# One run of all four P chunks over eight PSUM banks, and four blocks ahead of the seventh product

## The chip, the cores and the metric

The kernel runs on one core of a Trainium2 chip. The metric is the time of one execution on the device, in microseconds. Five engines work side by side, each on its own queue in order: TensorE (PE, with weight loads shown as PEld), VectorE (DVE), ScalarE (ACT), GpSimd (POOL) and SyncE (SP, which here only issues DMAs).

## The reference

For each of 8 batches and 8 heads, 512 rows of x and 32 rows of state (64 wide) read each other by softmax attention. The 544 result rows per batch, 8 heads side by side (512 wide), go through a two-layer network with an exact Gelu.

```
scores = scale * x @ state.T;   a  = softmax(scores);   xread = a  @ state
scores2 = scale * state @ x.T;  a2 = softmax(scores2);  sread = a2 @ x
h = concat(xread, sread) as (B*544, 512) @ w_in         # w_in 512 x 2048
out = gelu(h) @ w_out                                   # w_out 2048 x 512
```

## The kernel before

The kernel never forms xread. For a batch b it multiplies the state with `w_in` first (P, 128 rows x 2 x 2048), and then `h = a @ P`. The work of a batch is:

- `scores`, `norm`: exponentials and normalized weights `a`; `xtr_dma` and `atr_dma` transpose x and `a` by DMA from the SP queue.
- `p_mm(b, f, tiles)` (line 423): one of four column chunks f of P. It fills two PSUM tiles (t = 0, 1) of 128x512 with 8 matmuls of 64 rows x 32 columns each. `p_copy` (line 438) brings tile 0 to SBUF with ACT (L440) and tile 1 with DVE (L441).
- `mm1` (line 489), called by `M(..)`: one of 16 blocks of h, 2 matmuls of 128x512 (L494) and a Gelu on ACT (L501). "Block 8" is m = 8.
- `X(b, name)` (line 621): one of seven products of a Strassen scheme for `gelu(h) @ w_out`, 16 matmuls of 128x256 each (L591). Products 3 and 5 share PSUM bank 0, products 4 and 2 bank 1, products 1 and 7 bank 2, and product 6 has bank 3. `g_sum` (line 582) makes the sums of blocks that a product needs, on DVE (L585). X3 is copied by ACT (L635), X5 by ACT (L643), X2 by ACT (L648). POOL forms `u` (L646) and `v` (L610) from SBUF. DVE adds `v` and bank 3 (L618), and `u` and X7 (L654); after each of these and after X5 a DMA on SP writes part of the output (L605).
- `sread` (line 386): the state's read of x, 32 small matmuls into one PSUM tile `sr` (L392); `sread_out` normalizes it on DVE straight out of PSUM (L405, L406). `srt` transposes it on PE (L416), and DVE copies it (L419).

PSUM has eight banks: four `f` buffers that go round in the order of allocation (`ftile`, used by h blocks, `sr`, `srT`, scores and P chunks), and four fixed banks `o0` to `o3` (`otile`, used by the products, and by P chunks in between).

The order is written out by hand: each engine's queue holds its instructions in the order of the program text. The main loop (line 1116) runs over batches b = 2 to 7, and in each over eight positions p. A "slot" here is one pass of b. In slots 2 to 6, each p issues blocks 2p and 2p + 1. Products 4, 5, 1, 2, 7 of the previous batch come at p = 0 to 4, and products 3 and 6 of batch b at p = 6 and 7. P of the next batch is made in two runs, chunks 0 and 1 at p = 5 and chunks 2 and 3 at p = 7. In slot 2 two chunks of batch 2's own P are still to be made, by `pmat(2, 2)` at p = 0 and `pmat(2, 3)` at p = 3, in `f` buffers. In slot 6 the reads of batches 6 and 7 are both made. In slot 2, `hold_for` (L912) is a tiny POOL copy that waits for block 12's Gelu before POOL issues the load of x 5.

Of the kernel before, what the change touches and what calls it, by code (L numbers as in the profile page):

```python
# [9 lines left out]
FP32 = mybir.dt.float32  # L10
BF16 = mybir.dt.bfloat16
# [6 lines left out]
def kernel(  # L18
# [36 lines left out]
    def otile(shape, name, at=None):  # L55
        if at is None:
            at = turn[0] % 4
            turn[0] += 1
        return ps_o.tile(shape, FP32, name=name, tag=f"o{at}")

    def ftile(shape, name):
        return ps_f.tile(shape, FP32, name=name, tag="f")
# [323 lines left out]
    def sread(b):  # L386
        A = atts[b]
        A.sr = ftile([128, 2, 65], "sr")
        for t in range(2):
            for j in range(SJ):  # L390
                for c in range(HC):
                    nc.tensor.matmul(  # L392
                        A.sr[32 * c:32 * c + 32, t, :],
                        lhsT=A.e[:, 2 * j + t, 32 * c:32 * c + 32],
                        rhs=A.xo[:, j, c, 1 + 65 * t:66 + 65 * t],
                        start=(j == 0),
                        stop=(j == SJ - 1),
                    )

    def sread_out(b):  # L400
        A = atts[b]
        A.srm = att.tile([128, 2, D], BF16, name="srm", tag="srm")
        flat = A.sr.rearrange("q t d -> q (t d)")
        inv = att.tile([128, 2], FP32, name="inv", tag="inv")
        nc.vector.reciprocal(out=inv, in_=flat[:, 0:130:129])  # L405
        nc.vector.tensor_tensor(  # L406
            out=A.srm,
            in0=flat[:, 1:129].rearrange("q (t d) -> q t d", t=2),
            in1=inv[:, :].to_broadcast((128, 2, D)),
            op=ALU.mult,  # L410
        )
# [26 lines left out]
    def p_copy(b, f, ps):  # L438
        dst = Ps[b][:, :, f * 512:(f + 1) * 512]
        nc.scalar.copy(out=dst[:, 0, :], in_=ps[0])  # L440
        nc.vector.tensor_copy(out=dst[:, 1, :], in_=ps[1])  # L441
# [140 lines left out]
    def g_sum(b, name):  # L582
        (h0, k0), (h1, k1), op = G_SUMS[name]
        t = apool.tile([128, MH, 256], BF16, name="gsum", tag="gsum")
        nc.vector.tensor_tensor(out=t, in0=g_q(b, h0, k0), in1=g_q(b, h1, k1), op=op)  # L585
        xs[b, "g" + name] = t
# [34 lines left out]
    def X(b, name):  # L621
        bank = {"3": 0, "4": 1, "5": 0, "2": 1, "1": 2, "6": 3, "7": 2}[name]
        first = name in "3416"
        if first:
            xs[b, bank] = otile([128, 2, NH], "xp", bank)
        ps = xs[b, bank]
        lhs = {"3": (0, 0), "4": (1, 1)}.get(name)
        lhs = xs[b, "g" + name] if lhs is None else g_q(b, *lhs)
        rhs = {"5": w_q[1][1], "2": w_q[0][0]}.get(name)
        rhs = w_sum[name] if rhs is None else rhs  # L630
        x_mm(ps, lhs, rhs, first)
        if name == "3":
            xs[b, "s3"] = c_tile("s3")
            if b > 1:
                nc.scalar.copy(out=xs[b, "s3"], in_=ps)  # L635
            for h in range(2):
                xs[b, "o", h] = hpool.tile([128, 2, d_model], FP32, name="oh", tag=f"oh{h}")
        elif name == "4":
            xs[b, "s34"] = c_tile("s34")
            nc.vector.tensor_tensor(out=xs[b, "s34"], in0=ps, in1=xs[b, "s3"], op=ALU.add)  # L640
        elif name == "5":
            o = xs[b, "o", 0][:, :, NH:]
            nc.scalar.copy(out=o, in_=ps)  # L643
            xs[b, "u"] = c_tile("u")
            x_out(b, 0, right)
            nc.gpsimd.tensor_tensor(out=xs[b, "u"], in0=xs[b, "s34"], in1=o, op=ALU.subtract)  # L646
        elif name == "2":
            nc.scalar.copy(out=xs[b, "o", 1][:, :, :NH], in_=ps)  # L648
            c22(b)
        elif name == "1":  # L650
            xs[b, "q"] = c_tile("q")
            nc.vector.tensor_tensor(out=xs[b, "q"], in0=ps, in1=xs[b, "s34"], op=ALU.add)
        elif name == "7":
            nc.vector.tensor_tensor(  # L654
                out=xs[b, "o", 0][:, :, :NH], in0=ps, in1=xs[b, "u"], op=ALU.add
            )
            x_out(b, 0, left)
# [88 lines left out]
    def sr_w(name):  # L746
        if name in "52":
            homes = [opool.tile([128, 2, 512], BF16, name="srw", tag="osb") for _ in range(2)]
        elif name == "7":
            t = att.tile([128, 2, 2, 512], BF16, name="srw7", tag="xT")  # L750
            homes = [t[:, 0], t[:, 1]]
        else:
            t = x4s["16".index(name)].rearrange("p j c n -> p (j c n)")
            t = t.rearrange("p (g k f) -> p g k f", g=2, k=2)
            homes = [t[:, 0], t[:, 1]]
        (h0, k0), (h1, k1), op = G_SUMS[name]
        for g in range(2):
            nc.vector.tensor_tensor(
                out=homes[g], in0=sr_wq(h0, k0, g), in1=sr_wq(h1, k1, g), op=op
            )  # L760
            sr["w" + name, g] = homes[g]
# [133 lines left out]
            nc.vector.tensor_tensor(out=rs["o", 0][:, :NH], in0=ps, in1=rs["u"], op=add)  # L895
            r_out(0)

    def p_run(b, fs, banks, copy=None):
        done = []
        for f, at in zip(fs, banks):  # L900
            it = iter(at or ())
            tiles = (lambda shape, name: otile(shape, name, next(it))) if at else ftile
            done.append((b, f, p_mm(b, f, tiles)))
        for x in done:
            (copy or p_copy)(*x)

    def p_copy_v(b, f, ps):
        for t in range(2):
# [207 lines left out]
    for b in range(2, B):  # L1116
        nb = b + 1
        for p in range(8):
            k = 16 * b + 2 * p
            if p == 1 and nb < B:  # L1120
                scores(nb, 0)
                scores(nb, 1)
            if p in (2, 3) and nb < B:
                norm(nb, p - 2)
            if p == 3 and nb + 1 < B:
                xtr_dma(nb + 1)
            if p == 5 and nb < B:
                atr_dma(nb)
            if p == 7 and nb < B:
                srt(b)  # L1130
                if nb == B - 1:
                    srt(nb)
            if nb == B and p < 5:
                read_out_slot(p)
                if p == 4:
                    r_homes()
                    r_sum("5")
                    r_sum("2")
                continue
            M(k, k + 1)  # L1140
            if b == 2 and p in (0, 3):
                pmat(2, 2 + p // 3)
            if b == 2 and p == 1:
                w_sums(4)
            if p < 5:
                if p == 0:
                    g_sum(b - 1, "5")
                    if b > 2:
                        sr_w("5216"[b - 3])
                X(b - 1, "45127"[p])  # L1150
                if p < 3:
                    g_sum(b - 1, "127"[p])
            if p == 0 and b + 3 < B:
                hold_for(b, 0)
                load_x(4 if b == 2 else b + 3)
            if p == 6 and b == 2:
                hold_for(b, 12)
                load_x(5)
            if p == 0 and nb + 1 < B:
                begin(nb + 1)  # L1160
                rearr(nb + 1)
            if nb == B:
                if p == 5:
                    g_sum(b, "6")
                    R("3")
                    r_sum("1")
                    R("4")
                    r_sum("6")
                    r_sum("7")
                if p == 6:  # L1170
                    R("5")
                    X(b, "3")
                    R("2")
                    R("1")
                if p == 7:
                    R("6")
                    X(b, "6")
                continue
            if p == 5:
                g_sum(b, "6")  # L1180
                reads = (b, nb) if nb == B - 1 else (b,)
                for r in reads:
                    sread(r)
                p_run(nb, (0, 1), ((0, 1), (3, 2)))
                for r in reads:
                    sread_out(r)
                if b == 2:
                    rearr_ones(3)
                elif nb + 1 < B:
                    rearr_ones(nb + 1)  # L1190
            if p == 6:
                X(b, "3")
            if p == 7:
                if b == 2:
                    rearr_ones(4)
                p_run(nb, (2, 3), ((1, 2), None))
                X(b, "6")
    b = B - 1
    for name in "521":
# [39 lines left out]
```

## Time and profile before

| | |
|---|---|
| median of 3 runs | 203.81 us (203.44 to 204.97) |
| profiled execution, from the first to the last instruction | 202.5 us |
| PE busy | 196.6 us (97%) |
| DVE busy | 157.1 us (78%) |
| ACT busy | 135.4 us (67%) |
| POOL busy | 67.9 us (34%) |
| granted TensorE clock | 1.000 |
| share of PE in the chain that ended last | 89% |
| L429, P matmuls | 248, 10.5 us busy |
| L440 / L441, copies of P | 29 each, 599 ns / 683 ns |

The busy time of PE is a union of the matmuls' spans; they are pipelined, so the start of a group to the start of the next tells what a group costs. The chain that ended last is followed back from the last instruction, at each step to what released it or to the instruction before it on its engine. In the timeline each line has a start, a length up to the end of the last instruction of the group, the engine, the source line, the operation, the tiles and the count, and in brackets the idle time before it and what ended that. Of the profiled execution the page gives the span alone. The median of the runs is 1.3 us longer.

### The profile page before, as it was taken

The numbers are of one execution on the slowest core, as the hardware profiler recorded it, in microseconds if no ns is written. First come the engines' busy times: TensorE is split into PE (matmuls) and PEld (weight loads), VectorE is DVE, ScalarE is ACT, GpSimd is POOL, SyncE is SP. The second block draws the span as 40 slices with busy tenths as digits, with TensorE's granted clock in tenths as the row PEclk, the third lists the DMA queues.
The fourth block names the chain that finished last, engine by engine and source line by source line (L and its number), as shares of the span: only waits on it lengthen the run. The fifth ranks groups of instructions, "written<-read, shape, count | busy, mean of one in ns | idle before, by whom it ended". The sixth has DMA issues, their size and how long they took to land.

```text
span 202.5 us, 4900 instructions
## 1 busy us (share of the span) xinstructions
PE 196.6 (97%) x2035; PEld 132.6 (65%) x2035; DVE 157.1 (78%) x255; ACT 135.4 (67%) x240; POOL 67.9 (34%) x75
## 2 busy tenths in 40 slices
PE   7898999999999999999999999999999999999994
PEld 2433544465667577766776687567775787878893
DVE  2953776789998979878897787768778988895882
ACT  3785577699885779566967596687847576864120
POOL 8962603323249555360627502430220002200000
PEclk9999999999999999999999999999999999999999
DMA  6999999977675788782774308440107001040125
GB/s 203 174 174 203 205 199 197 181 134 142 96 135 107 207 104 108 155 179 32 90 163 142 77 0 123 130 119 0 52 9 202 3 0 55 0 159 0 52 102 162
DMA packets 40566, 23.16 MB, mean 114 GB/s; under 512 B 21856, under 2 KB 39136, under 8 KB 40544
## 3 DMA queue, kind: packets, MB, share of 16 engines
q0 software_dynamic: 13984, 8.10, 29.3%
q1 hardware_dynamic: 25872, 14.36, 28.5%
q10 hardware_dynamic: 688, 0.39, 0.6%
q8 instruction: 16, 0.26, 0.5%
q14 instruction: 6, 0.05, 0.1%
HBM read 17.30 MB, written 8.91 MB: 129 GB/s over the span
## 4 chain that ended last, share of the span: by engine, by line
PE 89%; DMA 5%; POOL 4%; DVE 0%; issue 0%; POOLq 0%
PE xp L591 41%; PE hp L494 26%; DMA xb<-in_x_dram 5%; PE p_ps L429 4%; PE op L536 4%; PE sp L798 3%; PE rp L864 3%; POOL w_in_bf L105 2%; PE op L520 2%; PE xp L703 2%; PE pt L333 2%; PE sr L392 1%; POOL sbd L95 1%; POOL w_out_bf L113 1%; PE xT_ps L271 1%; POOL st_bf L121 0%
## 5 line engine op out<-in xcount | busy, mean ns | idle before, releaser
L501 ACT ACTIVATE g<-hp 128x512 bf16<-128x512 f32 x124 | 67.1, 605 | 27.9 <-PE hp L494 21.3
L494 PE MATMUL hp<-AT,P 128*128 128x512 bf16 x248 | 62.9, 379 | 0.0
L591 PEld LDWEIGHTS <-gsum 128*128 128x128 bf16 x528 | 51.0, 98 | 12.1 <-issue 1.9
L585 DVE TENSOR_TENSOR gsum<-g 128x2048 bf16<-128x2048 bf16 x35 | 45.5, 1314 | 0.1
L591 PE MATMUL xp<-ws,gsum 128*128 128x256 bf16 x304 | 36.3, 273 | 0.0
L494 PEld LDWEIGHTS <-P 128*128 128x128 bf16 x248 | 22.8, 98 | 20.5 <-issue 2.7
L591 PE MATMUL xp<-ws,g 128*128 128x256 bf16 x224 | 26.8, 273 | 0.0
L591 PE MATMUL xp<-w_out_bf,gsum 128*128 128x256 bf16 x224 | 26.6, 273 | 0.0
L591 PEld LDWEIGHTS <-g 128*128 128x128 bf16 x224 | 21.7, 98 | 4.6 <-issue 0.2
L646 POOL TENSOR_TENSOR u<-s,oh 128x512 f32<-128x512 f32 x6 | 8.8, 1466 | 41.1 <-ACT oh L643 41.1
L441 DVE CAST P<-p_ps 128x512 bf16<-128x512 f32 x29 | 18.7, 683 | 3.1 <-PE p_ps L429 2.9
L440 ACT CAST P<-p_ps 128x512 bf16<-128x512 f32 x29 | 15.8, 599 | 5.4 <-PE p_ps L429 5.1
L225 POOL COPY x<-xb 128x1024 bf16<-128x1024 bf16 x12 | 12.6, 1080 | 15.7 <-DMA xb<-in_x_dram 15.7
L235 POOL COPY xo<-xb 128x1024 bf16<-128x1024 bf16 x12 | 14.5, 1234 | 4.6 <-PE sr L392 4.6
L610 POOL TENSOR_TENSOR v<-q,oh 128x512 f32<-128x512 f32 x6 | 8.6, 1434 | 20.6 <-ACT oh L648 20.5
L536 PE MATMUL op<-w_out_bf,g 128*128 128x512 bf16 x48 | 11.8, 380 | 0.0
L356 DVE TENSOR_TENSOR a<-e,ics 128x512 bf16<-128x512 bf16 x14 | 10.7, 764 | 0.5
L429 PE MATMUL p_ps<-w_in_bf,sbd 64*32 64x512 bf16 x248 | 10.5, 382 | 0.0
L353 DVE TENSOR_REDUCE cs<-e 128x16 f32<-128x512 bf16 x14 | 9.5, 677 | 0.7 <-ACT e L340 0.7
L419 DVE COPY XSR<-srT 128x128 bf16<-128x128 bf16 x8 | 5.7, 759 | 5.5 <-PE srT L416 5.5
L501 ACT ACT_TABLE_LOAD x7 | 9.0, 1283 | 0.1
L618 DVE TENSOR_TENSOR oh<-xp,v 128x512 f32<-128x512 f32 x6 | 4.1, 690 | 5.2 <-POOL v L610 5.2
(132 smaller groups left out, 230.2 us busy)
## 6 DMA issues: line engine op xcount, KB each, us to landing
out_dram<-oh SPq DMA_DIRECT2D x15, 256.0 KB, 2.9
xb<-in_x_dram POOLq DMA_DIRECT2D x7, 512.0 KB, 5.9
out_dram<-oh SPq DMA_DIRECT2D x6, 512.0 KB, 2.9
w_in_bf<-in_moe_w_in_dram POOLq DMA_DIRECT2D x6, 256.0 KB, 12.4
out_dram<-osb SPq DMA_DIRECT2D x5, 256.0 KB, 3.2
w_out_bf<-in_moe_w_out_dram POOLq DMA_DIRECT2D x4, 256.0 KB, 8.9
w_out_bf<-in_moe_w_out_dram POOLq DMA_DIRECT2D x2, 512.0 KB, 13.3
x0f<-in_x_dram SPq DMA_DIRECT2D x3, 256.0 KB, 3.7
```

The costliest lines, as they stand in the source:

```text
L225: nc.gpsimd.tensor_copy(out=A.x4[:, :, :, 64 * t:64 * t + 64].rearrange("p j c d -> p c j d"), in_=src[:, t],)
L235: eng.tensor_copy(out=A.xo[:, :, :, 2 + 64 * t:66 + 64 * t].rearrange("p j c d -> p c j d"), in_=src[:, t],)
L353: nc.vector.reduce_sum(out=cs, in_=e4, axis=AX.X)
L356: nc.vector.tensor_tensor(out=A.a[:, :, hs].rearrange("p g (c n) -> p g c n", n=NS), in0=e4, in1=ics[:, :, :].to_broadcast((128, G, 2, NS) ...
L429: nc.tensor.matmul(ps[t][32 * c:32 * c + 32, :], lhsT=sbd[64 * t:64 * t + 64, b, c, 32 * t:32 * t + 32], rhs=w_in_bf[64 * t:64 * t + 64, c ...
L440: nc.scalar.copy(out=dst[:, 0, :], in_=ps[0])
L441: nc.vector.tensor_copy(out=dst[:, 1, :], in_=ps[1])
L494: nc.tensor.matmul(hp, lhsT=Ps[b][:, t, m * 128:(m + 1) * 128], rhs=atts[b].AT[:, :, t, :], start=(t == 0), stop=(t == 1),)
L501: nc.scalar.activation(out=gs[b][:, m, :], in_=hp, func=AF.Gelu)
L536: nc.tensor.matmul(ops[b, j], lhsT=gs[b][:, m, j * 128:(j + 1) * 128], rhs=w_out_bf[:, m, :], start=(m == 0), stop=(m == MC - 1),)
L585: nc.vector.tensor_tensor(out=t, in0=g_q(b, h0, k0), in1=g_q(b, h1, k1), op=op)
L591: nc.tensor.matmul(ps[:, j - js[0], :], lhsT=lhs[:, m, 128 * j:128 * j + 128], rhs=rhs[:, m, :], start=(first and j == js[0] and m == 0), ...
```

## The change

- A new `p_all` takes the place of `p_run`. At p = 5 it issues the reads (`reads_mm`), then all four chunks of the next batch's P, in tiles (o0, f), (f, f), (o1, o3), (o2, f), then all eight copies, and then the normalization of the reads (`reads_norm`). The run at p = 7 is gone.
- `reads_mm` copies the raw reads out of PSUM with ACT into an SBUF tile `sraw`; `reads_norm` works from that tile.
- Product 7 of the previous batch moves from p = 4, behind blocks 8 and 9, to p = 5, behind blocks 10 and 11.
- `g_sum(b, "6")` moves from p = 5 to p = 3, ahead of product 2.
- Product 3 of batch b moves from p = 6, behind blocks 12 and 13, to p = 5, directly behind the P run.

```diff
-    def p_run(b, fs, banks, copy=None):
+    def reads_mm(bs):
+        sr = ftile([128, len(bs), 2, 65], "sr")
...
+        raw = cpool.tile([128, len(bs), 130], FP32, name="sraw", tag="sraw")
+        nc.scalar.copy(out=raw, in_=sr.rearrange("q i t d -> q i (t d)"))
+        return raw
+
+    def reads_norm(bs, raw):
...
+            nc.vector.reciprocal(out=inv, in_=raw[:, i, 0:130:129])
+            nc.vector.tensor_tensor(
+                out=A.srm,
+                in0=raw[:, i, 1:129].rearrange("q (t d) -> q t d", t=2),
...
+    def p_all(b, bs):
+        raw = reads_mm(bs)
         done = []
-        for f, at in zip(fs, banks):
-            it = iter(at or ())
-            tiles = (lambda shape, name: otile(shape, name, next(it))) if at else ftile
+        for f, at in enumerate(((0, None), (None, None), (1, 3), (2, None))):
+            it = iter(at)
+
+            def tiles(shape, name):
+                i = next(it)
+                return ftile(shape, name) if i is None else otile(shape, name, i)
+
             done.append((b, f, p_mm(b, f, tiles)))
         for x in done:
-            (copy or p_copy)(*x)
+            p_copy(*x)
+        reads_norm(bs, raw)
...
-            if p < 5:
+            if p < 4 or (p == 4 and nb == B):
...
+                if p == 3:
+                    g_sum(b, "6")
                 X(b - 1, "45127"[p])
...
             if p == 5:
-                g_sum(b, "6")
+                X(b - 1, "7")
                 reads = (b, nb) if nb == B - 1 else (b,)
-                for r in reads:
-                    sread(r)
-                p_run(nb, (0, 1), ((0, 1), (3, 2)))
-                for r in reads:
-                    sread_out(r)
+                p_all(nb, reads)
                 if b == 2:
                     rearr_ones(3)
                 elif nb + 1 < B:
                     rearr_ones(nb + 1)
-            if p == 6:
                 X(b, "3")
             if p == 7:
                 if b == 2:
                     rearr_ones(4)
-                p_run(nb, (2, 3), ((1, 2), None))
                 X(b, "6")
```

More of the change, by code (lines that the diff above doesn't have):

```diff
@@ L896, in R @@
             r_out(0)
-    def p_run(b, fs, banks, copy=None):
-        done = []
-        for f, at in zip(fs, banks):
-            it = iter(at or ())
-            tiles = (lambda shape, name: otile(shape, name, next(it))) if at else ftile
+    def reads_mm(bs):
+        sr = ftile([128, len(bs), 2, 65], "sr")
+        for i, b in enumerate(bs):
+            A = atts[b]
+            for t in range(2):
+                for j in range(SJ):
+                    for c in range(HC):
+                        nc.tensor.matmul(
+                            sr[32 * c:32 * c + 32, i, t, :],
+                            lhsT=A.e[:, 2 * j + t, 32 * c:32 * c + 32],
+                            rhs=A.xo[:, j, c, 1 + 65 * t:66 + 65 * t],
+                            start=(j == 0),
+                            stop=(j == SJ - 1),
+                        )
+        raw = cpool.tile([128, len(bs), 130], FP32, name="sraw", tag="sraw")
+        nc.scalar.copy(out=raw, in_=sr.rearrange("q i t d -> q i (t d)"))
+        return raw
+    def reads_norm(bs, raw):
+        for i, b in enumerate(bs):
+            A = atts[b]
+            A.srm = att.tile([128, 2, D], BF16, name="srm", tag="srm")
+            inv = att.tile([128, 2], FP32, name="inv", tag="inv")
+            nc.vector.reciprocal(out=inv, in_=raw[:, i, 0:130:129])
+            nc.vector.tensor_tensor(
+                out=A.srm,
+                in0=raw[:, i, 1:129].rearrange("q (t d) -> q t d", t=2),
+                in1=inv[:, :].to_broadcast((128, 2, D)),
+                op=ALU.mult,
+            )
+    def p_all(b, bs):
+        raw = reads_mm(bs)
+        done = []
+        for f, at in enumerate(((0, None), (None, None), (1, 3), (2, None))):
[3 more added lines that the diff above has]
+                return ftile(shape, name) if i is None else otile(shape, name, i)
             done.append((b, f, p_mm(b, f, tiles)))
         for x in done:
-            (copy or p_copy)(*x)
+            p_copy(*x)
+        reads_norm(bs, raw)
     def p_copy_v(b, f, ps):
```

## The prediction

> **What bounds the kernel now.** I read the busy rows of the page first, then the chain that ended last, then the timelines of TensorE (PE), ScalarE (ACT) and VectorE (DVE) over slots 2, 4 and 6. All times are from the profiled execution.
>
> ```profile
> span 202.5 us, 4900 instructions
> PE   7898999999999999999999999999999999999994
> PEclk9999999999999999999999999999999999999999
> ```
>
> PE is full from the fifth slice to the last but one, at full clock. So any edit in the slots counts only by what PE does, or waits for, more or less. The chain in order of time (start, length, what), slot 4 from its `X(.., "2")` to the next slot:
>
> ```profile
> 103.75 1.75 PE xp L591 x16
> 105.50 0.86 PE hp L494 x4
> 106.36 1.75 PE xp L591 x16
> 108.11 0.86 PE hp L494 x4
> 108.97 0.36 PE sr L392 x29
> 109.33 0.56 PE p_ps L429 x16
> 109.89 0.97 PE hp L494 x4
> 110.86 1.75 PE xp L591 x16
> 112.60 0.06 PE srT L416
> 112.66 0.86 PE hp L494 x4
> 113.52 0.56 PE p_ps L429 x16
> 114.08 1.85 PE xp L591 x16
> ...
> 156.52 0.88 PE p_ps L429 x16
> ```
>
> The chain is PE alone: no other engine ends a wait there. What follows a P run is longer by 0.10 to 0.11 (0.97 against 0.86, 1.85 against 1.75), the price of leaving the run. The last line is the second run of slot 6, 0.88 instead of 0.56: 0.32 of waiting for a PSUM buffer.
>
> ```profile
> 109.73 1.07 ACT L440 CAST P<-p_ps 128x512 bf16<-128x512 f32 x2
> 112.70 0.58 ACT L635 COPY s<-xp 128x512 f32<-128x512 f32 x1 [0.90 <-PE srT L416]
> 107.95 0.69 DVE L618 TENSOR_TENSOR oh<-xp,v 128x512 f32<-128x512 f32 x1 [1.16 <-POOL v L610]
> 110.29 1.28 DVE L441 CAST P<-p_ps 128x512 bf16<-128x512 f32 x2
> 63.85 0.68 DVE L441 CAST P<-p_ps 128x512 bf16<-128x512 f32 x1
> 62.65 1.03 PE L494 MATMUL hp<-AT,P 128*128 128x512 bf16 x4
> ```
>
> These are timeline rows. The first ACT copy of a run begins 0.47 after the run's first matmul (109.73 against 109.26, its timeline start). DVE has a hole of 1.16 before L618. The last two rows are slot 2: the DVE copy of `pmat(2, 3)` ends only at 64.53, while blocks 8 and 9 start at 62.65.
>
> **The change part by part.**
>
> *One P run less per slot, five slots.* In the PE timeline a run of two chunks lasts 0.56 from its first start to the next group's (109.26 to 109.82), a run of one chunk 0.34 (60.55 to 60.89). A chunk is therefore 0.22, and the rest belongs to the run. Before the second run the block pair takes 0.95 (112.50 to 113.45) instead of 0.86, and X6 behind it 1.76 instead of 1.75. Taken away: 0.56 + 0.09 + 0.01 = 0.66. Added to the first run: 2 x 0.22 = 0.44. That is -0.22 a slot before any wait.
>
> *Bank 0.* X3 now follows the run directly, and it writes the bank of the run's first tile. That tile is free when its ACT copy is done: 0.47 + 0.60 (mean of L440, 599 ns) + 0.05 to reach PE (ACT's copy of AT ended at 10.61, the matmul that waited began at 10.66) = 1.12 after the start of the run. PE is ready at 0.56 + 0.44 = 1.00. So X3 waits 0.12; formerly the pair of blocks 12 and 13 stood between. The new raw copy of `sr` goes ahead on ACT and has no row. The nearest are 0.26 (L198, 64x128) and 0.585 (128x512); for 130 columns I take 0.27, near the first, since 128x256 takes 0.37 (L874). The reads end 0.07 after the run's start and ACT is then idle, so the raw copy is over by 0.40, before the P copy can start. At 0.585 the P copy would begin at 0.61 and X3 would wait 0.26. With a bank freed early X3 waits nothing. Ends: -0.12 to +0.14 a slot around my value.
>
> The Trainium skill, page "TensorEngine Tiling (Array Packing)", section on the PSUM bottleneck, speaks against the change: tiling speeds up the matmuls but not the emptying of PSUM, so the copies may become the limit. The rows: eight copies at a step of 0.48 (ACT) and 0.60 (DVE) last until 2.95 after the run's start, against 1.00 for the matmuls. If all that follows had to wait for all eight, each slot would lose 1.95 and the time would be about 213; by the rows only X3's bank and the buffers below count.
>
> *Blocks 10 and 11 ahead of X7: slot 2.* The four `f` buffers go round. In slot 2 `pmat(2, 3)` takes two of them in p = 3, so block 11 gets the buffer that the DVE copy frees at 64.53 (64.58 at PE). Block 11 now wants to start three blocks of 0.43 behind 62.65, at 63.95: a wait of 0.63. Before, X7 stood between. What is late then is X7 and all behind it by 0.63. In slots 3 to 6 blocks 4 to 7 were the last users, long read: no wait. Blocks 8 to 11 also put `sr` after X7, at the same time as before (entry 0.09 either way).
>
> *X3 ahead of blocks 12 and 13.* X3's ACT copy (L635) now stands in front of their Gelus. Counted from the run: X3 from 1.12 to 2.87, its copy from 3.13, Gelu 12 from 3.61 to 4.22 (step 0.48, 0.60 long), buffer at PE 4.27, Gelu 13 0.48 later. Block 15 reuses block 12's buffer and would start at 4.23: 0.04 in slots 2 to 5. In slot 6 there are two `srT`, which shift the round by one: block 14 (wanted at 3.85) waits for Gelu 12, 0.42, and block 15 another 0.04. On the other side the 0.32 of slot 6's second run is gone. In slot 2 the POOL `hold` behind Gelu 12 and the load of x 5 come some 2.7 later (69.33 to about 72). With 5.9 to landing, and 2.02 of L225, the rearrangement ends about 80.0; `u` starts at 80.2. Nothing on the path.
>
> *DVE.* `g_sum(b, "6")` (1.21) goes ahead of L618, which waits for POOL until 107.95 anyway: it fits 106.79 to 107.95. In slot 2 the row was 1.80 beside POOL; then L618 ends about 66.9, when X7's add is not yet due. Behind L654 stand four copies (from 0.47, step 0.60, end 2.95), then reciprocal and product, end 3.36. `srT` wants that at 3.73. If that 0.37 of cover went, `srT` would wait one for one. L654 frees bank 2 about 0.5 after the run's start, and the fourth chunk wants it at 0.67.
>
> *SP.* X7's output now stands behind the AT transposition, which can go about 0.6 earlier; the output (2.9 to landing) is awaited only by X5's copy some 10 us later. Nothing.
>
> *Sum.* 5 x (0.44 + 0.12 - 0.66) = -0.50. Slot 2: +0.63. Block 15: 4 x 0.04 = +0.16. Slot 6: +0.46 - 0.32 = +0.14. Together +0.43 on the span of 202.5. The median is 203.81, 1.3 above the span, and nothing in that 1.3 is touched: 204.2.
>
> **The rivals.**
>
> *No new wait counts (faster).* Only the runs are merged and slot 6 loses its 0.32: 5 x -0.22 - 0.32 = -1.4, so 202.4. For it: PE has few releases on its path now. Against it: the copy that block 11 needs ends at 64.53 whatever PE does. Chance 0.13.
>
> *Bank 0 comes late (slower).* One mechanism: ACT's first P copy is released only with the end of the whole run. It then starts at 1.10, X3 at 1.75: 0.63 more a slot, 5 x 0.63 = 3.15 on top, 207.4. Against it: in slot 4 that copy began at 0.47, when chunk one was done and the second was running. It gives a loss over 1% once the copy starts later than 0.79 after the run's start (0.32 more a slot). Chance 0.08.
>
> *DVE falls behind.* The moved sum and POOL's `v` slow each other (L610 takes 1.27 to 1.68 in slots 3 to 6, a POOL row of this form 2.23 in slot 2). At 2.23 L654 frees bank 2 at 0.59, still below 0.67. Beyond that every 0.1 costs 0.1 in each slot; 0.2 each gives 205.2. Chance 0.09.
>
> That the order isn't what the text says is out: in the built program the run, X3 and the blocks stand as described.
>
> **How the numbers follow.** Forecast 204.2, chance 0.70. Its own range: bank 0 between 5 x -0.12 and 5 x +0.14; the Gelu waits of 0.62 between nothing and half as much again; slot 2's 0.63 from nothing. That is 203.0 with the first two low, 202.4 with all three, and 205.2 with all high. I give 202.8 to 205.3, which takes in the DVE rival. About 1% (2 us) is what a measurement of this kernel can tell from no change. The first rival stays within 1%, the second is over it, the third mostly within: faster 0.02, same 0.90, slower 0.08.
>
> **What would show it.** Right: one P group of 32 matmuls a slot, about 1.1 long to X3's start; in slot 2 a wait of block 11 for L441 of some 0.6; in slot 6 a wait of block 14 for a Gelu of some 0.4; slots 3 to 5 each shorter by 0.05 to 0.1. Wrong: X3 starting at 1.0 (then the first rival), or at 1.4 and more after the run's start (the second), or PE waiting for L654 or L618 inside the run (the third), or slot 2 without its wait.

## The result and the profile after

The changed kernel takes 205.24 us (median of 13 runs) against 203.79 for the kernel before: ratio 1.0064, 95% interval 1.0047 to 1.008. That is slower by 0.6%, clear of the noise, and inside both the forecast range (202.8 to 205.3, near its upper end) and the band of 1%. The forecast was 204.2: the direction was right, the size about a third of the measured one.

The page of the changed kernel, its span, its PE slices and the engine shares of the chain that ended last:

```profile
span 203.2 us, 4901 instructions
...
PE   7899999999999999999999999999999999999993
...
PE 68%; DVE 15%; DMA 5%; POOL 4%; issue 4%; ACT 2%; DVEq 0%; POOLq 0%; ACTq 0%
```

The slices still look full. The chain does not: PE had 89% of it before, now DVE has 15%. The busy row hides waits of a few tenths; the chain names who ended them.

PE's timeline after (start, length, line, operation; in brackets the idle time and what ended it), slots 2 to 6:

```profile
62.00 1.46 PE L494 MATMUL hp<-AT,P 128*128 128x512 bf16 x6
63.87 0.59 PE L494 MATMUL hp<-AT,P 128*128 128x512 bf16 x2 [0.40 <-DVE P L441]
...
87.80 0.99 PE L429 MATMUL p_ps<-w_in_bf,sbd 64*32 64x512 bf16 x24
88.99 0.41 PE L429 MATMUL p_ps<-w_in_bf,sbd 64*32 64x512 bf16 x8 [0.19 <-DVE oh L654]
...
109.48 0.84 PE L429 MATMUL p_ps<-w_in_bf,sbd 64*32 64x512 bf16 x24
110.48 0.41 PE L429 MATMUL p_ps<-w_in_bf,sbd 64*32 64x512 bf16 x8 [0.15 <-DVE oh L654]
...
112.58 1.03 PE L494 MATMUL hp<-AT,P 128*128 128x512 bf16 x4
113.72 0.23 PE L416 MATMUL srT<-ident,srm 128*128 128x128 bf16 x1
...
131.22 1.06 PE L429 MATMUL p_ps<-w_in_bf,sbd 64*32 64x512 bf16 x32
132.33 1.91 PE L591 MATMUL xp<-ws,g 128*128 128x256 bf16 x16
...
156.46 0.36 PE L416 MATMUL srT<-ident,srm 128*128 128x128 bf16 x2
156.99 1.10 PE L494 MATMUL hp<-AT,P 128*128 128x512 bf16 x4 [0.17 <-ACT g L501]
```

The bracketed idle times are shorter than the delays, because a matmul's row goes on while the next one waits; starts tell more. In slot 2, block 11 waits for the DVE copy L441, as forecast. In slots 3 and 4 the fourth chunk waits for DVE's add of X7 (L654), which frees bank 2; that was not in the sum. From the run to X3 it is 1.53 in slot 3 and 1.34 in slot 4. Also in slot 4, `srT` starts at 113.72, 0.28 later than the two blocks ahead of it (0.86 from 112.58) would let it. In slot 6, block 14 waits for a Gelu, as forecast. Where the run has no such wait, in slot 5, X3 starts 1.11 after it (131.22 to 132.33; forecast 1.12).

To compare executions I use the starts of the scores (L333) in PE's timeline, which mark one point in each slot, and for the rest the time from slot 6's scores to the start of the last DVE add:

| slot | before | after | change | by the prediction's sum |
|---|---|---|---|---|
| 2 | 21.80 | 22.32 | +0.52 | -0.10 + 0.63 + 0.04 = +0.57 |
| 3 | 21.34 | 21.68 | +0.34 | -0.06 |
| 4 | 21.34 | 21.74 | +0.40 | -0.06 |
| 5 | 21.34 | 21.25 | -0.09 | -0.06 |
| rest, slot 6 in it | 59.85 | 59.89 | +0.04 | +0.04 |
| sum | | | +1.21 | +0.43 |

The sum, +1.21, lies within the measured 1.0 to 1.6 (0.47% and 0.8% of 203.8). The spans differ by only 0.7 because the part ahead of slot 2, which the change does not touch, was 0.65 shorter in the profiled execution after. (The prediction's 1.3 between the span and the median is no fixed part: it sets one execution's span against the median of others. In one and the same execution after, the time is 205.13 and the span 203.2. The sum is added to the median and is not touched by this.)

So the question is slots 3 and 4: 0.86 more than forecast, all of the miss. The chain of slot 4, in order of time:

```profile
106.93 1.31 DVE gsum L585
108.24 0.91 issue
109.15 0.68 DVE oh L618
109.83 0.60 DVE oh L654
110.42 2.39 DVE P L441 x4
112.81 0.08 DVE inv L921
112.92 0.75 DVE srm L922
113.67 0.04 issue
113.72 0.23 PE srT L416
```

DVE is now on the path without a break (the 0.91 called issue still belongs to the sum, whose row lasts until 109.22): the moved sum, the two adds, four copies, the normalization, and only then `srT`. DVE's timeline of the same execution:

```profile
81.24 1.76 DVE L356 TENSOR_TENSOR a<-e,ics 128x512 bf16<-128x512 bf16 x1
...
86.52 1.21 DVE L585 TENSOR_TENSOR gsum<-g 128x2048 bf16<-128x2048 bf16 x1
...
91.43 0.29 DVE L922 TENSOR_TENSOR srm<-sraw,inv 128x128 bf16<-128x128 f32 x1
...
106.93 2.29 DVE L585 TENSOR_TENSOR gsum<-g 128x2048 bf16<-128x2048 bf16 x1
...
112.92 0.74 DVE L922 TENSOR_TENSOR srm<-sraw,inv 128x128 bf16<-128x128 f32 x1
...
128.24 2.31 DVE L585 TENSOR_TENSOR gsum<-g 128x2048 bf16<-128x2048 bf16 x1
```

And POOL's:

```profile
77.48 3.75 POOL L225 COPY x<-xb 128x1024 bf16<-128x1024 bf16 x2 [1.21 <-DMA xb<-in_x_dram]
...
106.47 1.68 POOL L610 TENSOR_TENSOR v<-q,oh 128x512 f32<-128x512 f32 x1 [3.34 <-ACT oh L648]
...
111.49 2.03 POOL L225 COPY x<-xb 128x1024 bf16<-128x1024 bf16 x2
...
128.21 1.27 POOL L610 TENSOR_TENSOR v<-q,oh 128x512 f32<-128x512 f32 x1 [3.31 <-ACT oh L648]
```

In slots 4 and 5 the moved sum takes 2.29 and 2.31 instead of 1.21, and each time it starts while POOL's `v` runs. In slot 5 it begins 0.03 behind `v` and ends 1.07 after it: as if it had done its work only once `v` was over. In slot 3 the sum is not stretched (1.21); there the norm's product takes 1.76 beside POOL's copies of x 5 (0.98 before), and DVE comes to the sum late. In slot 4 the normalization takes 0.74, beside POOL's copies, instead of 0.29; in slot 3, with POOL idle, it takes 0.29 out of SBUF as well.

### The profile page after: what moved, and what is told of

The parts are those of the page before. It is cut to its first block, busy times and chain, and to the rows that moved or that the text cites. A ratio compares the mean times of both kernels' runs of the same rounds, so it can differ in the third digit from the quotient of the medians.

```text
span 203.2 us, 4901 instructions
## 1 busy us (share of the span) xinstructions
PE 196.0 (96%) x2030; PEld 133.9 (66%) x2035; DVE 162.9 (80%) x255; ACT 136.6 (67%) x245; POOL 68.4 (34%) x75
## 4 chain that ended last, share of the span: by engine, by line
PE 68%; DVE 15%; DMA 5%; POOL 4%; issue 4%; ACT 2%; DVEq 0%; POOLq 0%; ACTq 0%
PE xp L591 30%; PE hp L494 20%; DVE gsum L585 6%; DMA xb<-in_x_dram 5%; PE op L536 3%; PE sp L798 3%; PE rp L864 3%; POOL w_in_bf L105 2%; DVE P L441 2%; DVE a L356 2%; PE op L520 2%; PE xp L703 2%; PE p_ps L429 2%; DVE cs L353 1%; PE pt L333 1%
## 5 line engine op out<-in xcount | busy, mean ns | idle before, releaser
L501 ACT ACTIVATE g<-hp 128x512 bf16<-128x512 f32 x124 | 66.3, 606 | 21.5 <-PE hp L494 17.0
L494 PE MATMUL hp<-AT,P 128*128 128x512 bf16 x248 | 62.0, 379 | 0.6 <-DVE P L441 0.4
L585 DVE TENSOR_TENSOR gsum<-g 128x2048 bf16<-128x2048 bf16 x35 | 50.2, 1449 | 4.1 <-ACT g L501 4.0
L591 PEld LDWEIGHTS <-g 128*128 128x128 bf16 x224 | 21.5, 98 | 5.0 <-issue 1.6
L225 POOL COPY x<-xb 128x1024 bf16<-128x1024 bf16 x12 | 14.3, 1225 | 16.6 <-DMA xb<-in_x_dram 16.6
L441 DVE CAST P<-p_ps 128x512 bf16<-128x512 f32 x29 | 18.3, 681 | 1.2 <-PE p_ps L429 1.0
L440 ACT CAST P<-p_ps 128x512 bf16<-128x512 f32 x29 | 15.3, 597 | 4.8 <-PE p_ps L429 4.7
L235 POOL COPY xo<-xb 128x1024 bf16<-128x1024 bf16 x12 | 13.2, 1129 | 5.0 <-PE sr L905 5.0
L356 DVE TENSOR_TENSOR a<-e,ics 128x512 bf16<-128x512 bf16 x14 | 11.7, 833 | 0.5
L536 PE MATMUL op<-w_out_bf,g 128*128 128x512 bf16 x44 | 11.1, 380 | 0.5 <-issue 0.3
L429 PE MATMUL p_ps<-w_in_bf,sbd 64*32 64x512 bf16 x248 | 9.6, 381 | 0.3 <-DVE oh L654 0.3
L536 PEld LDWEIGHTS <-g 128*128 128x128 bf16 x48 | 4.1, 97 | 5.9 <-issue 1.1
```

Source lines behind the costliest of these rows:

```text
L225: nc.gpsimd.tensor_copy(out=A.x4[:, :, :, 64 * t:64 * t + 64].rearrange("p j c d -> p c j d"), in_=src[:, t],)
L235: eng.tensor_copy(out=A.xo[:, :, :, 2 + 64 * t:66 + 64 * t].rearrange("p j c d -> p c j d"), in_=src[:, t],)
L356: nc.vector.tensor_tensor(out=A.a[:, :, hs].rearrange("p g (c n) -> p g c n", n=NS), in0=e4, in1=ics[:, :, :].to_broadcast((128, G, 2, NS) ...
L429: nc.tensor.matmul(ps[t][32 * c:32 * c + 32, :], lhsT=sbd[64 * t:64 * t + 64, b, c, 32 * t:32 * t + 32], rhs=w_in_bf[64 * t:64 * t + 64, c ...
L494: nc.tensor.matmul(hp, lhsT=Ps[b][:, t, m * 128:(m + 1) * 128], rhs=atts[b].AT[:, :, t, :], start=(t == 0), stop=(t == 1),)
L501: nc.scalar.activation(out=gs[b][:, m, :], in_=hp, func=AF.Gelu)
```

## The experiments

Theory 1: DVE is pushed back by POOL, through the moved sum beside `v` (slots 4 to 6) and through POOL's later copies (slot 3); L654 and bank 2 come late, then the fourth chunk and `srT`. Theory 2: the queue of DVE is too long by itself, with X7's add right ahead of four copies. The ratios are against the kernel before, with 95% intervals; the slots as in the table above.

| run | ratio | slot 2 | 3 | 4 | 5 | rest |
|---|---|---|---|---|---|---|
| before | 1 | 21.80 | 21.34 | 21.34 | 21.34 | 59.85 |
| after | 1.0064 (1.0047 to 1.008) | 22.32 | 21.68 | 21.74 | 21.25 | 59.89 |
| e1_home | 1.003 (1.0001 to 1.0059) | 21.75 | 21.68 | 21.74 | 21.25 | 59.90 |
| e2_v_dve | 1.013 (1.0062 to 1.0199) | 23.13 | 22.15 | 21.73 | 21.25 | 59.90 |
| e3_hold | 1.0105 (1.0015 to 1.0196) | 23.43 | 21.40 | 21.73 | 21.25 | 59.90 |
| e4_all | 1.0151 (1.0091 to 1.0211) | 25.21 | 21.21 | 21.73 | 21.21 | 59.49 |
| e5_late_sum | 1.0109 (1.0057 to 1.016) | 22.32 | 21.25 | 21.95 | 21.25 | 60.75 |
| e6_norm_first | 1.0089 (1.0052 to 1.0125) | 22.24 | 22.09 | 22.10 | 21.25 | 59.89 |
| e7_xo4_early | 1.0072 (1.0031 to 1.0114) | 22.37 | 21.68 | 21.74 | 21.25 | 59.90 |
| e8_srt_bank | 1.0039 (1.0019 to 1.006) | 22.29 | 21.65 | 21.73 | 21.21 | 59.49 |
| e9_x7_back | 1.0047 (1.0027 to 1.0067) | 21.82 | 21.68 | 21.74 | 21.38 | 59.90 |
| e10_sum_first | 0.9972 (0.9954 to 0.999) | 21.84 | 21.22 | 21.21 | 21.21 | 59.40 |
| e11_sum_late3 | 0.9997 (0.9982 to 1.0013) | 21.83 | 21.40 | 21.66 | 21.21 | 59.40 |
| e12_sum_first_only | 1.0031 (1.0002 to 1.006) | 21.75 | 21.49 | 21.75 | 21.25 | 59.90 |

A slot from 3 on that an edit does not touch repeats to 0.01 or 0.02; that is why one profile is enough to read it, while the times need many runs: e2 to e7 have two to four each, so their ratios are rough. Slot 2 repeats less well: the DVE copy that block 11 waits for starts 9.72 to 10.11 after slot 2's scores in all profiles but those of e10 and e12, which move it.

**e1_home: the buffer of block 11.**

```diff
+    def pmat_o0(b, f):
+        at = iter((None, 0))
...
-                pmat(2, 2 + p // 3)
+                (pmat_o0 if p == 3 else pmat)(2, 2 + p // 3)
```

`pmat_o0` is `pmat` with tile 1, the one that DVE copies, in bank o0.

> The changed kernel with one edit: in slot 2 the DVE half of pmat(2, 3) goes to bank o0 instead of an f buffer, so block 11 no longer takes the buffer that the DVE copy frees late. Both theories on the other slots expect the same here: block 11's wait (0.56 in the profile after, four blocks in 2.29 instead of 1.73) is gone, slot 2 from block 8 to the next slot's block 0 falls from 10.96 to 10.40, the other slots stay (10.78, 10.84, 10.34, 11.12). Time about 0.5 below the changed kernel, 204.7. If the wait had another cause, slot 2 stays at 10.96.

Slot 2 fell by 0.57, the others stayed to the hundredth. The wait of block 11 is the `f` buffer that the late DVE copy holds: shown.

**e2_v_dve: `v` on DVE.**

```diff
-        nc.gpsimd.tensor_tensor(
+        eng = nc.vector if b < B - 2 else nc.gpsimd
+        eng.tensor_tensor(
             out=xs[b, "v"], in0=xs[b, "q"], in1=o[:, :, :NH], op=ALU.subtract
         )
```

> The changed kernel with one edit: the difference v of batches 1 to 5 is formed on DVE instead of POOL. Theory 1 (POOL's v and the moved sum of X6 stretch each other, 2.3 instead of 1.2, and so push DVE's X7 add, the release of bank 2, past the fourth chunk's start): the sum of X6 takes 1.2 in slots 4 to 6 although DVE has one instruction of 0.69 more, the waits of slot 4 (0.22 in the run, 0.27 before srT) shrink by at least 0.3 together; in slot 3, where v did not lie beside the sum, DVE has 0.6 more to do and the run's wait grows from 0.41 to about 1.0. Theory 2 (the queue of DVE is too long by itself, with X7's add right ahead of four copies): 0.6 more work on DVE makes the waits longer in slots 3 and 4 alike, and new ones of 0.3 to 0.5 appear in 5 and 6. Time: 205.3 to 205.5 by theory 1, 206.5 by theory 2.

DVE's timeline of this run, slot 4:

```profile
108.33 1.22 DVE L585 TENSOR_TENSOR gsum<-g 128x2048 bf16<-128x2048 bf16 x1
...
113.98 1.06 DVE L923 TENSOR_TENSOR srm<-sraw,inv 128x128 bf16<-128x128 f32 x1
```

Without POOL's `v` beside it the sum takes 1.22: the stretching comes from POOL, as theory 1 has it. The run of slot 4 has no wait for DVE any more, and no new waits came in slots 5 and 6, which theory 2 wanted. But slot 4 gained nothing. The normalization (L923 here), now at the very time of POOL's copies, takes 1.06, and `srT` waits 0.5 instead of 0.27. I had not expected this second place. Slots 2 and 3 lost by the added DVE work: slot 3 0.47 (0.6 expected), and slot 2 0.8, which I had not expected, since `v` itself took 1.52 beside POOL's copies there. That is in the main why the whole, 206.91, lies above what either theory had (205.3 to 205.5, and 206.5).

**e3_hold: the load of x 5 earlier.**

```diff
             if p == 6 and b == 2:
-                hold_for(b, 12)
+                hold_for(b, 8)
```

> The changed kernel with one edit: in slot 2 POOL's hold before the load of x 5 waits for block 8's Gelu instead of block 12's. Theory 1 (slot 3's wait comes from POOL: its copies of slot 2 and 3 lie later than before, beside DVE's sums, which take 3.2 and 2.1 instead of 1.2, and DVE enters the second half of slot 3 1.2 late): DVE is back in time, the run of slot 3 falls from 1.53 to about 1.1, slot 3 from 10.78 to 10.35. Theory 2: slot 3 stays within 0.1 of 10.78. Time 204.8 against 205.2.

Slot 3 fell from 21.68 to 21.40: the run to X3 from 1.53 to 1.25, not to 1.1. DVE was in time (the norm's product 0.99 instead of 1.76), and then the sum met `v` again, which DVE's and PE's timelines show:

```profile
86.38 2.29 DVE L585 TENSOR_TENSOR gsum<-g 128x2048 bf16<-128x2048 bf16 x1
```

```profile
74.17 1.04 PE L494 MATMUL hp<-AT,P 128*128 128x512 bf16 x4 [0.26 <-DMA AT<-a]
```

The second line is the price: the load, some 3.5 earlier, ran into the AT transposition, which took 7.3 from issue to landing (4.3 after the change), and slot 3's first block waited for AT. Slot 2 lost 1.1: 0.42 there, 0.48 ahead of `srT` (POOL's copies again lay beside the normalization, 1.09), and 0.22 at block 11, whose copy came later in this execution ahead of anything that the edit touches.

**e4_all: the three edits and srT in other banks.** The diffs of e1, e2 and e3, and this one:

```diff
-                srt(b)
+                srt(b, 2)
                 if nb == B - 1:
-                    srt(nb)
+                    srt(nb, 1)
```

`srt(b, 2)` takes bank o2 in place of an `f` buffer, `srt(nb, 1)` bank o1.

> The three edits of the other runs together, and srT in the banks o2 and o1 instead of f buffers, so that blocks 14 and 15 take the buffers of the run's copies and not those of blocks 12 and 13. Theory 1: no wait of slots 2 to 6 is left but X3's for bank 0 (0.05 to 0.12 each); slots 10.40, 10.32, 10.30, 10.30, 10.60: 2.1 less than after, 0.9 less than before; time 203.0 against 203.8 before, ratio 0.996. Theory 2: waits of 0.2 to 0.5 stay in the run in slots 3 to 6, time 204.2 or more.

Slots 3 and 5 are as expected and the rest falls by 0.40 (0.52 expected); the whole is not: slot 2 is at 25.21, as PE's timeline shows.

```profile
68.26 0.41 PE L432 MATMUL p_ps<-w_in_bf,sbd 64*32 64x512 bf16 x7 [0.51 <-DVE oh L631]
...
76.86 1.04 PE L506 MATMUL hp<-AT,P 128*128 128x512 bf16 x4 [2.20 <-DMA AT<-a]
```

Against the changed kernel, slot 2 lost 2.36 to the wait for AT and 1.10 in the run, where `v` on DVE (1.52) makes the add of bank 3 (L631 here) late, and won 0.57 at block 11. Slot 4 stayed at 21.73, by the normalization as in e2. So the combination failed at three places: AT, `v` on DVE in slot 2, and the normalization.

**e5_late_sum: the moved sum behind the run.**

```diff
-                if p == 3:
-                    g_sum(b, "6")
...
                 p_all(nb, reads)
+                g_sum(b, "6")
```

> The changed kernel with one edit: the sum of X6 stands behind the whole P run and its normalization on DVE, not ahead of product 2. From the scores of one slot to those of the next, the profile after has 22.32, 21.68, 21.74, 21.25 (slots 2 to 5). Theory 1 (the moved sum, stretched to 2.3 beside POOL's v, makes DVE's add of X7 and with it bank 2 late): the sum takes 1.2 again, no matmul of a P run waits for DVE any more, slot 3 falls by 0.4 to 21.3, slot 4 loses the 0.2 of its run and most of the 0.3 ahead of srT; X6 may wait up to 0.5 for its sum in slot 4, where POOL's copies lie beside it. Theory 2 (the run's waits come from eight copies in a row, and DVE's queue is too long whatever stands ahead): slots 3 and 4 keep waits of 0.2 to 0.4 in the run.

This is the clearest test of the run's waits. With the sum out of the way, no chunk waits for DVE in any slot, and slot 3 is at 21.25, 0.43 lower, though x 5 is as late as after the change and the eight copies are the same. The waits for bank 2 come from the moved sum: shown, and the eight copies as their cause (theory 2) are out. How the sum does it differs: in slot 4 by its stretched 2.3 (e2 and e12 keep it ahead of the run at 1.2, and the wait is gone), in slot 3 by its plain 1.21 on a DVE that comes late. What e5 cost elsewhere: in slot 4 the normalization beside POOL's copies (1.06, `srT` 0.5 late) and X6 0.2 late for its sum; and at the end of slot 6 a wait that I had not foreseen, for the copy of `srT`, since the sum now stands ahead of it:

```profile
PE hp L494 <- DVE XSR L419: 0.8, 1, 0.8
```

(The waits of PE: who waited for whom, the sum, the count, the longest.)

**e6_norm_first: the normalization ahead of the copies.**

```diff
+        reads_norm(bs, raw)
         for x in done:
             p_copy(*x)
-        reads_norm(bs, raw)
```

> The changed kernel with one edit: the two DVE instructions that normalize the reads stand ahead of the four copies of P, not behind them. They are then done about 1.3 after the run's start, and srT wants them at 3.7. Both theories: the wait of srT in slot 4 (0.27) and of the second srT in slot 6 (0.07) is gone; the copies are 0.45 later, which delays block 14's buffer: at most 0.1 in slots 3 and 4. Slot 4 21.74 to 21.5; the run's own waits stay. If instead srT waits for something else than the normalization, slot 4 stays.

In slot 4 `srT` no longer waits, as expected. But my price for the later copies was wrong, 0.1 expected and 0.45 and 0.64 measured: block 14 waits for the fourth copy, in PE's waits

```profile
PE hp L494 <- DVE P L441: 1.1, 3, 0.5
```

because L654 is already late there, and the normalization, now beside POOL's copies in slot 3 too, took 0.96.

**e7_xo4_early: POOL's copies of x 4 ahead of the load of x 5.**

```diff
                 if b == 2:
                     rearr_ones(3)
+                    rearr_ones(4)
```

> The changed kernel with one edit: in slot 2 POOL's copies of x 4 (L235) stand ahead of the hold and the load of x 5, not behind them. Theory 1 (slot 3's wait comes from DVE being pushed back by POOL's later copies): the sum of X5 at the start of slot 3's period takes 1.2 instead of 3.2, DVE is some 1.5 earlier in slot 3 and the run's wait there falls from 0.41 to 0.25 or less (not to nothing: with DVE in time the moved sum again lies beside v); slot 2 may gain a wait ahead of srT of up to 0.3, since the copies now lie beside the normalization. Slot 3 21.68 to 21.45. Theory 2: slot 3 unchanged, the run's wait 0.4.

The sum of X5 came down from 3.17 to 1.23, and slot 3 did not move at all. That part of theory 1 fell: DVE only waited longer for X4 afterwards. What makes DVE late in slot 3 is the next thing, POOL's copies of x 5, which wait for their load (L225 at 77.98 here, 77.48 after, 75.88 before) and lie beside the norm's product. e3 moved that load and did help.

**e8_srt_bank: srT in o2 and o1.**

```diff
             if p == 7 and nb < B:
-                srt(b)
+                srt(b, 2)
                 if nb == B - 1:
-                    srt(nb)
+                    srt(nb, 1)
```

> The changed kernel with one edit: srT goes to bank o2 (the second one of slot 6 to o1) and takes no f buffer. Blocks 14 and 15 then take the buffers of the run's copies. Both theories: the 0.34 of block 14 in slot 6 and the 0.04 of block 15 in slots 2, 3 and 5 are gone, slot 6 with what follows 62.97 to 62.55; all other waits stay. If block 14 waits for something other than block 12's Gelu, 62.97 stays.

The two transposes of slot 6 with blocks 14 and 15 took 1.47 after (0.53 + 0.94) and 1.06 here; the rest fell from 59.89 to 59.49. Block 14 waits because `srT` turns the round of `f` buffers so that it needs block 12's: shown. (The 62.97 of the expectation reached to the end of the span, with the last DMA's landing in it; by that measure it was 62.85, as the landing took 0.3 longer.)

**e9_x7_back: product 7 back at p = 4.**

```diff
-            if p < 4 or (p == 4 and nb == B):
+            if p < 5:
...
-                X(b - 1, "7")
                 reads = (b, nb) if nb == B - 1 else (b,)
```

> The changed kernel with one part undone: product 7 stands at p = 4 again, behind blocks 8 and 9, and blocks 10 and 11 directly ahead of the reads. Slot intervals from scores to scores after: 22.32, 21.68, 21.74, 21.25. Both theories: block 11's wait in slot 2 is gone (-0.57). The Gelus of blocks 10 and 11 now end only about 0.4 after the run's start; the second chunk waits about 0.25 for block 11's buffer, the first copy of P starts 0.1 later and X3 waits a little longer: +0.3 in each slot. DVE's add of X7 comes 0.86 earlier where DVE is free; the theory that the moved sum pushes it expects slots 3 and 4 to keep their waits for bank 2, since DVE is late there through the sum and not through X7: 22.0, 21.9, 21.9, 21.55. If X7's late end is what made bank 2 late, slots 3 and 4 fall to 21.5.

Slots 3 and 4 stayed at 21.68 and 21.74 to the hundredth, though X7 ended 0.86 earlier. DVE's timeline says why:

```profile
106.25 2.29 DVE L585 TENSOR_TENSOR gsum<-g 128x2048 bf16<-128x2048 bf16 x1
108.46 0.68 DVE L618 TENSOR_TENSOR oh<-xp,v 128x512 f32<-128x512 f32 x1
109.06 0.67 DVE L654 TENSOR_TENSOR oh<-xp,u 128x512 f32<-128x512 f32 x1
```

L654 stands right behind L618 and the sum; X7's end does not matter to it. The expected 0.3 a slot for the Gelus of blocks 10 and 11 was only 0.13 in slot 5 and lay under the DVE wait in 3 and 4. For this kernel, then, moving the four blocks ahead bought 0.13 in slot 5 and cost 0.5 in slot 2.

**e12_sum_first_only: the sum ahead of the second norm.**

```diff
-            if p in (2, 3) and nb < B:
-                norm(nb, p - 2)
+            if p == 2 and nb < B:
+                norm(nb, 0)
...
                 if p == 3:
                     g_sum(b, "6")
+                    norm(nb, 1)
```

> The changed kernel with one edit: the sum of X6 stands ahead of the second norm at p = 3, not behind it; nothing is added or left out on DVE. Theory (the sum beside POOL's v is what makes bank 2 late in slot 4): the sums of X6 of slots 4 to 6 take 1.2 instead of 2.3, the run of slot 4 has no wait for bank 2, and srT's wait there goes too, since DVE is about 0.5 earlier: 21.74 to 21.35. In slot 3 POOL's v comes early and DVE is late through the load of x 5; there the sum can meet v and the run's wait stays: 21.7 or more. If the waits of slot 4 come from DVE's length alone, slot 4 stays at 21.74. Time 204.8.

The sums are at 1.2 and the run of slot 4 has no wait, as expected; slot 4 still took 21.75, not 21.35. The wait changed its place once more, to the normalization (DVE's timeline):

```profile
111.94 1.08 DVE L922 TENSOR_TENSOR srm<-sraw,inv 128x128 bf16<-128x128 f32 x1
```

DVE was earlier, so L922 lay fully beside POOL's copies (110.85 to 112.88) instead of at their end. In slot 2 the wait of block 11 went too, because the DVE copy that it waits for now stands ahead of the norm. Slot 3 fell to 21.49, where 21.7 or more was expected: the sum, now first, stayed at 1.2, and it was `v` that was held (1.27 after the change), as POOL's timeline shows:

```profile
84.33 2.21 POOL L610 TENSOR_TENSOR v<-q,oh 128x512 f32<-128x512 f32 x1 [2.33 <-DVE gsum L585]
```

Bank 2 still came late there: L654 ended 0.94 after the run's start (88.29 against 87.35), for 1.14 after the change.

**e10_sum_first: a version meant to beat both.** To e1, e6, e8 and e12 it adds a hold between the two that were tried:

```diff
             if p == 6 and b == 2:
-                hold_for(b, 12)
+                nc.gpsimd.tensor_copy(out=hold, in_=Ps[nb][:, 0, 2047:2048])
```

> A version meant to be faster than both: the half of pmat(2, 3) in bank o0, srT in o2 and o1, the normalization ahead of the four copies, POOL's hold of slot 2 behind the last ACT copy of P (the load of x 5 then goes about 2 earlier than after the change, and later than in the run where it met the AT transposition), and the sum of X6 ahead of the second norm, so that it lies ahead of POOL's v and not beside it. By the theory of DVE pushed back by POOL: sums of X6 at 1.2, no wait for bank 2 in slots 3 to 6; slots 21.65, 21.25, 21.25, 21.2, and the rest 0.4 below after; 0.8 below before: 203.0, ratio 0.996. If the load of x 5 still meets the transposition of AT, slot 2 or 3 gains a wait of 0.3 to 2 on AT.

203.22 against 203.69, ratio 0.9972 (0.9954 to 0.999): faster than the kernel before by 0.3%, and than the changed one by about 0.9%. Slots 3 to 5 came out within 0.04 of the expectation, the rest 0.49 below the changed kernel's (0.4 expected); slot 2 was 0.19 longer than expected (the run took 1.27 to X3, 0.1 more than after the change, as DVE's add of X7 ended only 0.88 after the run's start). The waits of PE that the view lists for the whole execution:

```profile
PE warm_ps L150 <- DVE warm L92: 1.2, 1, 1.2
PE op L548 <- issue: 0.3, 2, 0.2
PE hp L1058 <- ACT AT L376: 0.2, 1, 0.2
PE st_ps L180 <- ACT st_bf L176: 0.2, 1, 0.2
PE aT_ps L374 <- DVE a L315: 0.2, 1, 0.2
```

All of these are ahead of slot 2; shorter waits, as that of slot 2's run or bank 0's, are not in the list. A slot of 21.21 is 0.13 under the 21.34 of before: by the sum of the prediction (-0.22 + 0.12), about what the merged run is worth with bank 0's wait still in it.

**e11_sum_late3: a second such version.** e1, e6 and e8, and the sum behind the run in slot 3 alone:

```diff
-                if p == 3:
+                if p == 3 and b != 3:
                     g_sum(b, "6")
...
                 p_all(nb, reads)
+                if b == 3:
+                    g_sum(b, "6")
```

> A second version meant to be faster: the half of pmat(2, 3) in bank o0, srT in o2 and o1, the normalization ahead of the copies, and the sum of X6 behind the run in slot 3 alone. Slots 21.7, 21.25, 21.5 (bank 2 still 0.2 late, srT in time), 21.2, and the rest 0.4 below after: 0.55 below before, 203.2, ratio 0.997. If the normalization ahead of the copies makes block 15 wait for the fourth copy, slot 4 stays near 21.7.

Ratio 0.9997, no gain: slot 4 stayed at 21.66, with the fourth chunk late and block 15 0.2 late behind the fourth copy, and slot 3 at 21.40 (21.25 expected), as X6 came 0.18 late for its own sum behind the copies. Expected was 0.997.

## Why the prediction came out as it did

**Right, with sizes.** The direction, the merged run (1.11 to X3, forecast 1.12, bank 0's wait in it, with the copies going on until 2.99 in slot 5, forecast 2.95), the run saved in slot 5, block 11 (forecast 0.63, 0.56 measured, removed by e1), blocks 14 and 15 in slot 6 (forecast 0.46, 0.41 measured with the transposes, removed by e8). Slot 2 and the rest are within 0.05 of their sums, slot 5 within 0.03.

**Wrong: slots 3 and 4.** The sum had them 0.06 shorter each; they were 0.34 and 0.40 longer. The prediction's own sign for that, PE waiting for L654 inside the run, came in both. In slot 3 the run holds all of it (1.53 for 1.11); in slot 4 the run holds 0.23 of it and the wait ahead of `srT` 0.28, less the 0.04 of block 15. Three steps of the working failed.

**Wrong: the paragraph on DVE.** It let the sum of X6 into the hole of 1.16 ahead of L618 at its usual 1.21, because that hole was idle. It was idle for DVE but not for what DVE shares with POOL: the hole is there precisely because `v` runs. The sum took 2.3. I had seen a row of 1.80 for a sum beside POOL and used it for slot 2 only. L654 ended 0.95 after the run's start in slot 4 (110.43 against 109.48) where I had 0.5.

**Wrong: "nothing on the path" for the later load of x 5.** I had the copies of x 5 (L225) at 2.02 and asked only whether `u` is then in time. The copies took 3.75; `u` started at 81.19 behind them, about 1 later than I had it, and was still done 5.8 before L654 reads it. What counted was DVE: the norm's product, beside those copies, took 1.76. DVE was 1.1 later than before at its second norm and 1.35 later at the end of it (each from the slot's scores), and L654 ended 1.14 after the run's start (88.94 against 87.80).

**Wrong: the cover of `srT`.** I kept the 0.29 of the normalization although the change moves its input from PSUM to SBUF. In the kernel before, this product ran beside POOL's copies without harm, as DVE's and then POOL's timeline show:

```profile
111.68 0.29 DVE L406 TENSOR_TENSOR srm<-sr,inv 128x128 bf16<-128x128 f32 x1
```

```profile
109.30 2.96 POOL L235 COPY xo<-xb 128x1024 bf16<-128x1024 bf16 x2 [1.38 <-PE sr L392]
```

With both inputs in SBUF it took 0.74 beside them after the change, and up to 1.16 in the other runs (e6), but 0.29 with POOL idle. The copies took 2.96 here and 2.03 after the change: here a DVE sum (109.16, 1.21 long) had begun 0.14 ahead of them, and it was POOL's row that grew, and PE did not wait for it. After the change it was DVE's rows, for which PE waits. That the normalization out of PSUM would have saved `srT` in the changed kernel was not tried; e6, which puts it ahead of the copies, took the wait of `srT` away.

**The rivals.** The third, DVE falling behind, is what came on top, at a chance of 0.09. Its mechanism was half right: I let the sum stretch `v`, and it was `v` that held back the sum (in e12, with the sum first, it is `v` that is held). Its place was two slots, not five: in slots 5 and 6 the sum is just as long, but DVE comes in earlier there, and bank 2 is free in time. So it is partly luck that the time, 205.24, lies just inside the range: the upper end was worked out from the bounds of other terms and from 0.2 in each of five slots, not from 0.4 to 0.46 in two. The first and second rival did not happen.

The Trainium skill, page "SBUF — State Buffer", section "Who interferes with whom", states the rule: a DVE instruction with two inputs in SBUF contends with a GpSimd instruction that reads SBUF, because its second input comes through a read port that the two share, and the shared pair of ports is "an exclusive lock"; with at most one input in SBUF, outside its 2-port modes, a DVE instruction does not contend. The runs agree: 2.31 for the sum begun 0.03 after `v`, ended 1.07 after it; 1.22 with no `v` on POOL; 0.29 for the normalization out of PSUM beside POOL's copies, 0.50 to 1.16 out of SBUF. Its length there is what was left of the copy that POOL was making, and 0.14 more: 0.74 with 0.60 left after the change (112.92 to 113.52), 1.08 with 0.94 left in e12.

## What to carry to other kernels

When a step moves into an idle gap of an engine, ask what that gap waits for: a gap that waits for POOL has POOL busy in it, and a DVE sum of two SBUF tensors then gains little by starting early (here 2.31 for 1.21, ended 1.07 after POOL). A copy out of PSUM that frees a bank early also changes what its reader competes with. And where one engine's queue is nearly full, take a wait away only after following that queue to its end: here it came back as bank 2, as `srT`, as block 14 or as AT, until five edits together left slots 3 to 5 with bank 0's wait alone, and slot 2's run 0.1 too long.

## What the runs showed of the hardware that was not expected

A DVE row can grow from 0.29 to 1.16, or from 1.21 to 2.31 (and to 3.17 beside POOL's copies), from the place of its inputs and from what POOL does at that time; four copies out of PSUM kept their step of 0.60 (2.47 for four) in each slot, beside POOL's copies too. Which of the two is held can't always be read from the starts: the sum of 3.17 began 0.05 ahead of POOL's copies (72.24 against 72.29), which kept their 2.03. The load of x 5, issued at 67.9 instead of 71.4, delayed the AT transposition that was on its way: from issue to landing that took 3.5 before the change, 4.3 after it, 7.3 in e3 and 8.1 in e4, and 3.7 in e10, where the load was issued at 68.9, 2.45 behind the transposition. Slot 3's first block waited 0.26 in e3 and 2.2 in e4 (0.42 and 2.36 by the starts). The second is longer because in e4 the transposition itself was issued some 1.0 later in the slot, on SP's queue behind the output that waits for `v` on DVE, and landed 0.8 more slowly.
